# Attention's values in 32-column tiles turned by VectorE, a planner with other durations, and other banks where the channel products change

## The chip, the cores and the metric

The kernel runs on one core of one Trainium2 chip. A core has TensorE (PE) for matrix products, VectorE (DVE), ScalarE (ACT) and GpSimd (POOL) for elementwise work, and SyncE (SP), which here only issues DMAs. Matrix products land in PSUM: 128 partitions by eight banks of 512 fp32 words, addressed in the kernel as `ps[:, bank, column]`. Everything else lies in one SBUF tile called `arena`. The metric is device time in microseconds (us), lower is better; the median of several executions is compared.

## The reference, cut to what matters

```python
batch, n_heads, seq, head_dim = (4, 8, 768, 64);  n_clusters = 16
# routed attention, for each of 32 heads
q_assign = argmax(q_n @ c_n.T);  k_assign = argmax(k_n @ c_n.T)      # nearest centroid
scores = where(q_assign[:, None] == k_assign[None, :], q @ k.T / 8, -1e9)
attn = softmax(scores);  out = attn @ v
# x: (4, 768, 512), the heads side by side; then the mixer
h = relu(x.T @ w_tok1) @ w_tok2          # over tokens, 768 -> 256 -> 768
u = x + h.T
h2 = relu(u @ w_ch1) @ w_ch2             # over channels, 512 -> 1536 -> 512
return u + h2
```

The kernel reads the weights as pairs of 32-bit words (64-bit numbers) and rounds them on the chip; its products are fp32, the mask product bf16.

## The kernel before

**One program, planned.** The kernel first builds a list of operations with `g.add`: each has the engines it may run on with a cost in us for each, a function that issues its instructions, and the SBUF and PSUM pieces it reads and writes. `Program.run` gives each operation a due time, counted back from the TensorE operations that need it, and `Program.plan` then simulates the engines and picks, for each engine, the ready operation with the earliest due time. TensorE's operations stay in the order in which the program lists them; the order on VectorE, ScalarE, GpSimd and SyncE is what the plan yields. The constants `COST`, `LAT`, `LAND` and the costs written at each call are the plan's durations. On the chip each engine works through its list in that order and waits on semaphores.

**Attention** goes by pairs of heads, `m` from 0 to 15 (`NP`), two heads `h` on 64 partitions each. A pair has these steps on TensorE:
- `route(m + 2)`: which centroid each of 384 × 4 queries and keys is nearest to. Four products in 32-column tiles go to one bank; VectorE turns the bank in 32 × 32 blocks, takes maxima, compares and turns back; ScalarE makes a bf16 mask `rb`, which DMAs carry into `Ms`.
- `scores(m)`: 12 units, each of one half `u` of the queries (384 columns) and one block `i` of 128 keys. A unit has an fp32 product and a bf16 mask product per head, in two of the banks 0 to 5 (`2 * s + h`, `s = n % 3`). ScalarE's exponential moves each unit into a buffer `exs`; VectorE adds the exponentials over the blocks of keys into `es`.
- `values(m)`: for each unit and head one product with 64 columns of V as weights and 384 columns of exponentials moving, accumulated in banks 6 and 7 with head 0 on partitions 0 to 63 and head 1 on 64 to 127. So 24 products a pair. ScalarE copies the result to `avs`.
- `sums(m)`: four products with a 32-column matrix of ones give the softmax denominators in bank 5, which are copied to `denS`.
- `finish_x(m)`: nine transposes by TensorE (`turn`), six of `avs` into banks 6 and 7 and three of `denS` into bank 4, so that tokens lie on partitions; VectorE clamps and inverts the denominators and writes the quotient into `xs`, two products of 384 columns.

Beside this, `dma_turn_qk` prepares q and k of pair `m + 3`: ScalarE splits them in 16-bit halves, DMA transposes turn them, ScalarE puts them together again (`halves`). `weight_round` loads a piece of the weights and rounds it on VectorE (31 pieces), and `channel_weights` makes sums of the rounded pieces and stores them in DRAM (`wd1`, `wd2`).

**The mixer** follows: token products (`token1`, `token2`, in Winograd's form of Strassen's scheme with seven products for eight), then `channel1(grp)` and `channel2(grp)` for two groups of two batches. A channel `product` has seven steps of three matmuls; each step's result is taken out of its banks by VectorE, or by ScalarE where it is only copied. `channel1` alternates between banks 0 to 2 and 3 to 5, `channel2` uses one bank a step, chosen by the counter `nset[1]`. Between `channel1(1)` and `channel2(1)` stands `check()`, one tiny product and some vector operations that decide whether a general path has to run. At the end `store` turns four blocks of the output with TensorE, copies them out and sends them.

Two lines that the change touches in many places: TensorE's products all go through the helper `mm` (line 829 of the profile), and elementwise sums through `tt` (line 868), so these lines gather operations of every stage.

Of the kernel before, what the change touches and what calls it, by code (L numbers as in the profile page):

```python
# [14 lines left out]
ALU = mybir.AluOpType  # L15
# [5 lines left out]
P = 128  # L21
# [27 lines left out]
NEX = 11  # L49
# [4 lines left out]
    "ACT": (0.17, 0.00083),  # L54
    "ACT16": (-0.1, 0.00128),
    "DVE": (0.16, 0.00104),
# [8 lines left out]
LAND = 2.2  # L65


class Op:
    __slots__ = ("opts", "fn", "preds", "succs", "left", "ready", "end", "due", "seq", "eng", "lat", "bytes", "after", "port", "first_lat")


class Program:
# [5 lines left out]
    LAT = {"PE": 0.2, "ACT": 0.15, "DVE": 0.12, "POOL": 0.15, "SP": 0.0}  # L78
# [4 lines left out]
    def add(self, opts, fn, rd=(), wr=(), size=None, after=0.0):  # L83
# [3 lines left out]
        o.lat = 0.0  # L87
# [58 lines left out]
    def plan(self):  # L146
# [12 lines left out]
        order, at = [], {}  # L159
        while len(order) < len(ops):  # L160
            best = None
            for e in self.ENGINES:
                if e == "PE":
# [3 lines left out]
                    t = max(free[e], o.ready)  # L167
# [35 lines left out]
            if e == "PE":  # L203
                pe_at += 1
                at[o] = t
# [504 lines left out]
def kernel(  # L710
# [59 lines left out]
    rcps = [Buf(arena, 384 + 32 * i, [HJ, 4]) for i in range(2)]  # L770
    dall = Buf(arena, 448, [NP, HJ, 4])
# [55 lines left out]
    def mm(dst, lhsT, rhs, start, stop, cost, rd, wr, pos=None, tr=None):  # L827
# [6 lines left out]
        return g.add({"PE": cost}, fn, rd, wr)  # L834
# [46 lines left out]
    def vec(fn, c, rd, wr):  # L881
        return g.add({"DVE": c}, lambda e: fn(), rd, wr)
# [129 lines left out]
    def dma_turn_qk(m):  # L1012
# [11 lines left out]
        for n in range(2):  # L1024
            halves(dst[:, :, :, n], qkt[n].ap, 2 * S, qkt[n].k(), T.k())

    def route(m, bk):
# [4 lines left out]
        for gr in range(4):  # L1032
# [3 lines left out]
                T.ap[:, r0 : r0 + HJ].rearrange("p a t -> p (a t)"), True, True, 0.157,  # L1036
# [46 lines left out]
    def scores(m):  # L1083
        nonlocal nex
        T, M = Ts[m % 3], Ms[m % 2]
        st = unit[m] = []

        def plain(n):
            u, i = divmod(n, NJ)
            s, r0 = n % 3, NJ + HJ * u  # L1090
            for h in range(2):
# [3 lines left out]
                    T.ap[hs, r0 : r0 + HJ].rearrange("p a t -> p (a t)"), True, False, 0.316,  # L1095
# [8 lines left out]
        for n in range(2 * NJ):  # L1104
            u, i = divmod(n, NJ)
# [3 lines left out]
            for h in range(2):  # L1109
# [3 lines left out]
                    M.ap[hs, 0, u * HS : (u + 1) * HS], False, True, 0.078,  # L1113
# [3 lines left out]
            ex = exs[nex % len(exs)]  # L1117
            nex += 1
            st.append(ex)
            g.add(  # L1120
                {"ACT": 0.81},
# [783 lines left out]
```

## Time and profile before

| | us |
|---|---|
| median of 3 runs | 812.88 (812.24 to 814.05) |
| the profiled execution | 810.43 |
| its span, first to last instruction | 808.6 |
| TensorE busy | 788.8 (98% of the span) |
| VectorE busy | 672.1 (83%) |
| ScalarE busy | 474.7 (59%) |
| GpSimd busy | 179.3 (22%) |

Attention fills the first 343 us, token mixing follows up to the first "full" channel products, and the rest is channel products. In a row of groups stand the line, the engine, the operation, result and operands, the shape, the count, then busy time, mean duration in ns, and the idle time before with what ended it. In a row of the timeline stand start, duration, and in square brackets the idle time before. "PEld" is TensorE's loading of weights, which can overlap its matmuls; since the ends of matmuls are modelled, the starts tell the pace. A row of windows gives, for each stretch, the busy time of PE, PEld, DVE, ACT and POOL with the number of instructions, then the granted clock, the DMA share and GB/s.

### The profile page before, as it was taken

What the parts mean: (1) busy time and instruction counts of PE and PEld (TensorE: products, weight loads), DVE (VectorE), ACT (ScalarE), POOL (GpSimd) and SP (SyncE); (2) the same over time, 40 slices, a digit from 0 to 9 for tenths busy, and PEclk for the clock granted to TensorE, in tenths of its full rate; (3) what the DMA queues carried; (4) which work ended last, traced back from release to release, by engine and by line L of the source; (5) the groups of instructions that cost most, each with busy time, mean ns of one, the idle gap of its engine ahead of it and who ended that gap; (6) DMA issues with size and microseconds to landing.
All of it is one profiled execution on the core that took longest, in us unless ns stands there. A gap on an engine that the chain in (4) does not pass through costs nothing.

```text
span 808.6 us, 10858 instructions
## 1 busy us (share of the span) xinstructions
PE 788.8 (98%) x3743; PEld 428.0 (53%) x3743; DVE 672.1 (83%) x868; ACT 474.7 (59%) x613; POOL 179.3 (22%) x124
## 2 busy tenths in 40 slices
PE   5999999999999999999999999999999999999996
PEld 3454445444445554444555555555555555555553
DVE  4788999999999999998898876799974676789974
ACT  4588888888888875799913236433455505300423
POOL 1000000000000000000345498500196279610000
PEclk9999999999999999999999999999999999999999
DMA  6777678879887984369839765556899843333656
GB/s 135 225 173 177 181 196 201 219 184 220 198 218 176 231 236 105 90 137 211 146 97 253 208 192 184 177 182 198 243 231 263 220 117 107 89 102 103 177 146 151
DMA packets 265119, 143.49 MB, mean 177 GB/s; under 512 B 184288, under 2 KB 260960, under 8 KB 265056
## 3 DMA queue, kind: packets, MB, share of 16 engines
q1 hardware_dynamic: 262560, 141.88, 68.4%
q10 hardware_dynamic: 2496, 0.84, 0.4%
q8 instruction: 32, 0.52, 0.3%
q14 instruction: 31, 0.25, 0.1%
HBM read 91.95 MB, written 28.61 MB: 149 GB/s over the span
## 4 chain that ended last, share of the span: by engine, by line
PE 96%; DVE 1%; ACT 0%; issue 0%; DMA 0%; SPq 0%; ACTq 0%
PE ps L829 96%; DVE arena L850 0%; DVE arena L868 0%; DMA arena<-arena 0%; ACT arena L875 0%; ACT arena L1122 0%; ACT arena L848 0%; SPq L888 0%; DVE arena L1244 0%; DVE arena L1045 0%; DVE arena L1044 0%; ACTq L848 0%
## 5 line engine op out<-in xcount | busy, mean ns | idle before, releaser
L829 PE MATMUL ps<-arena 128*128 128x384 f32 (+6 forms) x3743 | 788.8, 463 | 12.5 <-DVE arena L981 5.7
L829 PEld LDWEIGHTS ps<-arena 128*128 128x128 f32 (+3 forms) x3359 | 408.6, 168 | 346.9 <-issue 142.6
L868 DVE TENSOR_TENSOR arena<-arena 128x1536 f32<-128x1536 f32 (+6 forms) x351 | 365.7, 1067 | 14.4 <-ACT arena L1122 7.5
L868 POOL TENSOR_TENSOR arena<-arena 128x384 f32<-128x384 f32 (+1 forms) x116 | 175.9, 1547 | 530.7 <-DVE arena L868 396.0
L868 DVE TENSOR_TENSOR arena<-ps,arena 128x384 f32<-128x384 f32 (+2 forms) x259 | 208.0, 810 | 81.5 <-PE ps L829 74.1
L858 ACT COPY arena<-arena 128x768 uint16<-128x768 uint16 (+1 forms) x197 | 191.7, 1050 | 47.0 <-DVE arena L868 29.6
L1122 ACT ACTIVATE arena<-ps 128x768 f32<-128x768 f32 x192 | 150.3, 810 | 16.7 <-PE ps L829 13.2
L848 ACT COPY arena<-ps 128x384 f32<-128x384 f32 (+2 forms) x68 | 45.9, 677 | 133.1 <-PE ps L829 123.1
L1755 ACT ACTIVATE arena<-arena 128x768 f32<-128x768 f32 x40 | 38.7, 967 | 59.8 <-DMA arena<-in_moe_w_ch_dram 43.1
L875 ACT ACTIVATE arena<-arena 128x1152 f32<-128x1152 f32 (+1 forms) x38 | 40.1, 1076 | 55.3 <-DVE arena L868 27.9
L829 PEld LDWEIGHTS <-arena 64*128 64x128 bf16 x384 | 19.3, 94 | 26.3 <-issue 1.8
L850 DVE COPY arena<-ps 128x384 f32<-128x384 f32 (+3 forms) x17 | 12.8, 774 | 15.2 <-PE ps L829 13.5
L1238 DVE SCALAR_TENSOR_TENSOR arena<-arena 128x512 uint32<-128x512 uint32 (+1 forms) x31 | 20.7, 672 | 0.3
L1244 DVE SCALAR_TENSOR_TENSOR arena<-arena 128x512 f32<-128x512 uint32 (+1 forms) x31 | 20.7, 691 | 0.2
L1044 DVE STREAM_TRANSPOSE arena<-ps 128x384 f32<-128x384 f32 x16 | 9.3, 584 | 13.6 <-PE ps L829 13.6
L1053 ACT ACTIVATE arena<-arena 128x384 bf16<-128x384 f32 x16 | 11.2, 703 | 10.3 <-DVE arena L1179 10.3
L1234 DVE TENSOR_SCALAR arena<-arena 128x512 uint32<-128x512 uint32 (+1 forms) x31 | 12.9, 440 | 0.0
L1241 DVE TENSOR_SCALAR arena<-arena 128x512 uint32<-128x512 uint32 (+1 forms) x31 | 12.7, 430 | 0.2
L1049 DVE STREAM_TRANSPOSE arena<-arena 128x384 f32<-128x384 f32 x16 | 9.2, 575 | 0.4
L1045 DVE TENSOR_REDUCE arena<-arena 128x24 f32<-128x384 f32 x16 | 8.8, 553 | 0.6
L1755 ACT ACTIVATION_READ_ACCUMULATOR arena<-arena 128x1 f32 x40 | 7.6, 190 | 0.0
L1186 DVE RECIPROCAL arena<-arena 128x12 f32<-128x12 f32 x16 | 3.6, 228 | 0.6
(47 smaller groups left out, 19.1 us busy)
## 6 DMA issues: line engine op xcount, KB each, us to landing
arena<-wd SPq DMA_DIRECT2D x196, 192.0 KB, 2.4
wd<-arena SPq DMA_DIRECT2D x84, 224.0 KB, 3.7
arena<-in_moe_w_ch_dram SPq DMA_DIRECT2D x48, 256.0 KB, 4.4
arena<-in_moe_w_ch_dram SPq DMA_DIRECT2D x16, 768.0 KB, 4.5
arena<-in_v_dram SPq DMA_DIRECT2D x16, 384.0 KB, 4.4
out_dram<-arena SPq DMA_DIRECT2D x14, 384.0 KB, 3.6
arena<-in_k_dram SPq DMA_DIRECT2D x13, 384.0 KB, 4.4
arena<-in_q_dram SPq DMA_DIRECT2D x13, 384.0 KB, 4.4
```

Source lines behind the costliest of these rows:

```text
L829: nc.tensor.matmul(dst, lhsT=lhsT, rhs=rhs, start=start, stop=stop, tile_position=pos, is_transpose=tr, skip_group_check=True,)
L848: nc.scalar.copy(out=dst, in_=src)
L850: nc.vector.tensor_copy(out=dst, in_=src)
L858: nc.scalar.copy(out=dst, in_=src)
L868: (nc.vector if e == "DVE" else nc.gpsimd).tensor_tensor(out=dst, in0=a, in1=b, op=op)
L875: nc.scalar.activation(out=dst, in_=src, func=ACT.Relu)
L1122: lambda e, ex=ex, s=s: nc.scalar.activation(out=ex.ap, in_=ps[:, 2 * s : 2 * s + 2, 0:HS], func=ACT.Exp, scale=SM_SCALE),
L1234: vec(lambda: nc.vector.tensor_scalar(out=hh, in0=hi, scalar1=0x07FFFFFF, scalar2=3, op0=ALU.bitwise_and, op1=ALU.logical_shift_left,), f, ...
L1238: vec(lambda: nc.vector.scalar_tensor_tensor(out=TT, in0=hi, scalar=0xC0000000, in1=hh, op0=ALU.bitwise_and, op1=ALU.bitwise_or), 0.14 + 0 ...
L1241: vec(lambda: nc.vector.tensor_scalar(out=hh, in0=TT, scalar1=0xFF800000, scalar2=None, op0=ALU.bitwise_and), f, T.k(), h.k())
L1244: vec(lambda: nc.vector.scalar_tensor_tensor(out=ll, in0=lo, scalar=float(2.0**-52), in1=hh.bitcast(F32), op0=ALU.mult, op1=ALU.mult,), 0. ...
L1755: lambda e, i=i, func=func, bias=bias, n=n, hi=hi: nc.scalar.activation(out=hi, in_=hi, func=func, bias=bias, accum_out=wsum.ap[:, i, n : ...
```

## The change

- **Values.** The tile has 32 columns of V instead of 64. For each block `i` there are 16 products: two heads, two halves of 32 channels, and four groups of queries; a group is every fourth run of 32 queries, so 192 columns move in runs of 32. The four groups go to the four 32-partition strips of a bank, so VectorE can turn the result in 32 × 32 blocks straight into `xs`, and `avs` and TensorE's transposes go.
- **Exponentials.** One buffer holds both halves of a block (seven buffers of 2 × 768). From pair 1 on, scores go block by block rather than half by half. `es` holds two partial sums over three blocks each; `sums` adds them in PSUM with eight products.
- **Order.** `route(m + 2)` stands between scores and values for pairs 2 to 13, after the finish for pairs 0 and 1; `sums` stand before the last block of values. The finish of the last pair no longer stands inside token mixing.
- **Planner.** Other costs and latencies, a cost for a change of TensorE's tile form (`SWITCH`), and one between dependent operations of one engine (`SELF`). Piece `n` of the weights may not be loaded before 14 + 12 n us of the plan. `halves` of 1536 elements are split in two.
- **Channel products.** `nset[1]` is set to 3 at the start of each `channel2`, the check's product moves from bank 7 to bank 0, two sums are split in two, and the stores of the last group are issued between the steps of the last product, into banks 4 to 7.

```diff
 COST = {
-    "ACT": (0.17, 0.00083),
-    "ACT16": (-0.1, 0.00128),
-    "DVE": (0.16, 0.00104),
+    "ACT": (0.09, 0.00083),
+    "ACT16": (-0.36, 0.001426),
+    "DVE": (0.075, 0.00104),
     "POOL": (0.12, 0.0023),
 }
+SWITCH = 0.1
+SELF = 0.13
+START, STEP = 14.0, 12
...
-    LAT = {"PE": 0.2, "ACT": 0.15, "DVE": 0.12, "POOL": 0.15, "SP": 0.0}
+    LAT = {"PE": 0.2, "ACT": 0.22, "DVE": 0.2, "POOL": 0.15, "SP": 0.0}
...
-                    t = max(free[e], o.ready)
+                    t = max(free[e] + (SWITCH if o.mode != mode else 0.0), o.ready)
...
-                s.ready = max(s.ready, o.end + (self.delay(o) if s.opts.keys() != {e} or o.lat else 0.03))
+                if e == "PE" and "PE" in s.opts:
+                    d = 0.0
+                elif s.opts.keys() == {e} and not o.lat:
+                    d = SELF if e in ("ACT", "DVE") else 0.03
+                else:
+                    d = self.delay(o)
+                s.ready = max(s.ready, o.end + d)
...
-    exs = [buf(48 + 3 * i, [2, HS]) for i in range(12)]
-    es = [buf(84 + 6 * i, [2, 2, HS]) for i in range(2)]
-    avs = buf(102, [2, HS])
-    denS = buf(105, [HS])
+    exs = [buf(48 + 6 * i, [2, S]) for i in range(6)] + [buf(96, [2, S])]
+    es = [buf(84 + 6 * i, [2, S]) for i in range(2)]
+    denT = buf(105, [HS])
...
-            halves(dst[:, :, :, n], qkt[n].ap, 2 * S, qkt[n].k(), T.k())
+            for r in range(0, NQK, NJ):
+                halves(
+                    dst[:, r : r + NJ, :, n], qkt[n].ap[:, r : r + NJ], S, qkt[n].k(),
+                    T.rows(r, r + NJ),
+                )
...
+        def chunk(n):
+            return divmod(n, NJ) if m == 0 else divmod(n, 2)[::-1]
...
-        for u in range(2):
-            a, e = es[u], st[NJ * u : NJ * u + NJ]
...
-            x, y, z = two(0), two(2), two(4)
-            tt(a.ap, x.ap, y.ap, ALU.add, 4 * HS, x.k() + y.k(), a.k())
-            tt(a.ap, a.ap, z.ap, ALU.add, 4 * HS, a.k() + z.k(), a.k())
-            tt(a.ap[:, 0], a.ap[:, 0], a.ap[:, 1], ALU.add, 2 * HS, a.k(), a.rows(0, 1))
+        for n in range(2):
+            a = es[n]
+            x, y, z = st[HJ * n : HJ * n + HJ]
+            tt(a.ap, x.ap, y.ap, ALU.add, 2 * S, x.k() + y.k(), a.k())
+            tt(a.ap, a.ap, z.ap, ALU.add, 2 * S, a.k() + z.k(), a.k())
...
+    def tokens(ap, gr):
+        return ap.rearrange("p (j t) -> p j t", t=P)[:, :, 32 * gr : 32 * gr + 32]
+
+    def values(m, i):
+        V, ex = vs[m % 3], unit[m][i]
+        mms(
+            [
+                (
+                    ps[32 * gr : 32 * gr + 32, 6 + h, c * HS // 2 : (c + 1) * HS // 2],
+                    V.ap[:, h, i, 32 * c : 32 * c + 32], tokens(ex.ap[:, h], gr),
+                    i == 0 and c == 0, i == NJ - 1, (0, 32 * gr),
+                )
+                for h in range(2) for c in range(2) for gr in range(4)
+            ],
+            1.29, V.k() + ex.k(), bank(6, 7), (P, 32),
+        )
...
     def sums(m, bk):
-        for u in range(2):
...
+        for n in range(2):
+            mms(
+                [
+                    (
+                        ps[32 * gr : 32 * gr + 32, bk, 0:HS], ones.ap,
+                        tokens(es[n].ap.rearrange("p h t -> p (h t)"), gr), n == 0, n == 1,
+                        (0, 32 * gr),
+                    )
+                    for gr in range(4)
+                ],
+                0.645, es[n].k() + ones.k(), bank(bk), (P, 32),
+            )
...
+        vec(lambda: nc.vector.transpose(out=denT.ap, in_=ps[:, bk, 0:HS]), 0.57, bank(bk), denT.k())
...
+        vec(
+            lambda: nc.vector.transpose(
+                out=x.ap[:, :, cols].rearrange("p j (c d) -> p c j d", d=32),
+                in_=ps[:, 6:8, 0:HS],
+            ),
+            0.96, bank(6, 7), xk,
+        )
+        xv = x.ap[:, :, cols].rearrange("p j (h d) -> p j h d", h=2)
+        tt(
+            xv, xv,
+            rcp.ap.rearrange("p h j -> p j h").unsqueeze(3).to_broadcast([P, NJ, 2, D]),
+            ALU.mult, S, xk + rcp.k(), xk,
+        )
+
+    def pair(m):
+        scores(m)
+        early = 2 <= m < NP - 2
+        if early:
             route(m + 2, 0)
-        sums(m, 5)
-        if 3 <= m + 3 < NP:
+        for i in range(NJ):
+            if i == NJ - 1:
+                sums(m, 5)
+            values(m, i)
+        finish_x(m, 5)
+        if m == 0:
+            load_v(2)
+            turn_qk(2, (1, 2, 3))
+        if m < 2:
+            route(m + 2, 0)
+        if m + 3 < NP:
             dma_turn_qk(m + 3)
...
+        after = START + STEP * npiece
         raw, (h, T, low) = raws[npiece % 3], tmps[npiece % 2 if npiece < 22 else 0]
...
-    nset = [0, 3]
+    nset = [0, 0]
...
+            for late in dict(then).get(n, ()):
+                late()
...
+        nset[1] = 3
         product(2, 2, Hm[1, 1], u[0, 1], u[0, 1], ("POOL",))
...
-        product(2, 3, Hm[1, 0], u[1, 0], u[1, 0])
+        stores = [
+            lambda f=f, hf=hf: store(grp, 0, f, hf) for f, hf in ((2, 1), (3, 1), (2, 0), (3, 0))
+        ]
+        then = {4: stores[0:1], 5: stores[1:2], 6: stores[2:4]} if grp else {}
+        product(2, 3, Hm[1, 0], u[1, 0], u[1, 0], then=then)
...
-        bk, o, queue = 2 + nost, ost[nost], ("SP", "ACT")[nost % 2]
+        bk, o, queue = 4 + nost, ost[nost], ("SP", "ACT")[nost % 2]
...
-        mm(ps[0:32, 7, 0:3], ones.ap, cnt.ap[:, 0:3], True, True, 0.1,
-           cnt.k() + ones.k(), bank(7), pos=(0, 0))
+        mm(ps[0:32, 0, 0:3], ones.ap, cnt.ap[:, 0:3], True, True, 0.1,
+           cnt.k() + ones.k(), bank(0), pos=(0, 0))
...
-    finish_x(NP - 1, (6, 7), 4)
```

More of the change, by code (lines that the diff above doesn't have):

```diff
@@ L48 @@
 W = 64
-NEX = 11
 SUM_LO, SUM_HI = 1e-15, 1e15
@@ L1602, in product @@
         )
-        for pn, (r, rk), st, fresh, part, more in seq:
+        for n, (pn, (r, rk), st, fresh, part, more) in enumerate(seq):
             w = ring[nring % len(ring)]
@@ L1819 @@
     for m in range(NP):
[L1820 to L1825 removed]
+        pair(m)
     load_token_weights()
```

165 lines of the change are left out of this document (60 added, 105 removed).

## The prediction

> **What bounds the kernel now.** I read the page first: its busy rows, the slices, the chain that ended last.
>
> ```profile
> PE 788.8 (98%) x3743; PEld 428.0 (53%) x3743; DVE 672.1 (83%) x868; ACT 474.7 (59%) x613; POOL 179.3 (22%) x124
> PE   5999999999999999999999999999999999999996
> PEclk9999999999999999999999999999999999999999
> PE 96%; DVE 1%; ACT 0%; issue 0%; DMA 0%; SPq 0%; ACTq 0%
> ```
>
> TensorE sets the time: 98% busy, 96% of the chain, its clock full. So an edit is worth what it takes out of TensorE's stream, and work of other engines counts only where it makes TensorE wait. "Busy" hides small losses, because the ends of matmuls are modelled and overlap; I therefore go by the starts of weight loads in the timeline. One pair of heads in mid-attention:
>
> ```profile
> 182.51 0.30 PEld L829 LDWEIGHTS ps<-arena 64*128 64x128 f32 x4 [0.17 <-issue]
> ...
> 192.40 0.20 PEld L829 LDWEIGHTS ps<-arena 128*64 128x64 f32 x4 [0.48 <-DVE arena L868]
> 192.78 0.14 PEld L829 LDWEIGHTS ps<-arena 128*64 128x64 f32 x2 [0.18 <-issue]
> ...
> 199.55 0.14 PEld L829 LDWEIGHTS ps<-arena 128*64 128x64 f32 x2 [0.18 <-issue]
> ...
> 200.29 0.16 PEld L829 LDWEIGHTS ps<-arena 128*32 128x32 f32 x8 [0.60 <-ACT arena L858]
> 200.46 0.80 ACT L848 COPY arena<-ps 128x768 f32<-128x768 f32 x1 [0.21 <-ACT arena L858]
> 200.64 0.13 PEld L829 LDWEIGHTS ps<-arena 128*32 128x32 f32 x4 [0.19 <-DVE arena L1241]
> 200.97 0.13 PEld L829 LDWEIGHTS ps<-arena 128*32 128x32 f32 x4 [0.19 <-issue]
> 201.21 0.58 DVE L1044 STREAM_TRANSPOSE arena<-ps 128x384 f32<-128x384 f32 x1 [0.75 <-PE ps L829]
> 201.72 1.03 PEld L829 LDWEIGHTS ps<-arena 128*128 128x128 f32 x9 [0.62 <-ACT arena L848]
> ...
> 202.92 0.30 PEld L829 LDWEIGHTS ps<-arena 64*128 64x128 f32 x4 [0.17 <-issue]
> ```
>
> The pair lasts 202.92 − 182.51 = 20.41 us: scores 9.89, values in 64-column tiles 7.89, route and sums in 32-column tiles 1.43, nine turns 1.20. Each part includes the step into the next form of tile. These parts are what the change rewrites.
>
> **The pace of small tiles.** The row of the value matmuls by form, and the token stage's 512-column stream:
>
> ```profile
> L829 PE MATMUL ps<-arena 128*64 128x384 f32 x768 | 127.4, 488 | 0.0
> 344.00 0.19 PEld L829 LDWEIGHTS ps<-arena 128*128 128x128 f32 x1 [0.24 <-issue]
> ...
> 347.86 0.19 PEld L829 LDWEIGHTS ps<-arena 128*128 128x128 f32 x1 [0.24 <-issue]
> ```
>
> The code issues 16 pairs × 24 = 384 value matmuls and the row has 768, so an fp32 matmul is two instructions. Two 64-column tiles run side by side: from 192.78 to 199.55 lie 21 steps, 0.3224 us for 384 columns. Between 344.00 and 347.86 lie nine steps of 512 columns, 0.4289. The slope is (0.4289 − 0.3224)/128 = 0.00083 us a column, the fixed part 0.003. Four 32-column tiles side by side (a quad, four instructions) also step by 0.33 for 384 columns (200.64 to 200.97). So a quad of 192 columns should take 192 × 0.00083 + 0.003 = 0.1626 us.
>
> **The change part by part, on TensorE.**
> - Values: 16 matmuls a block, six blocks a pair: 6 × 16 × 2 / 4 = 48 quads × 0.1626 = 7.80 us, against 24 steps × 0.3224 = 7.74. The cost is even (+0.06), though instructions go from 48 to 192 per pair.
> - Sums: eight matmuls of 384 columns instead of four, because VectorE no longer adds the two halves: four quads instead of two, 1.29 instead of 0.645 us.
> - Turns: nine a pair go, 1.20 us with the step out of them.
> - Form steps: values, sums and early route now share the 32-column form. A step costs 200.29 − 199.55 = 0.74 for two quads of work, 0.74 − 2 × 0.322 = 0.10; the 32-column part ends 1.43 − 4 × 0.3224 = 0.14 late, step out included. Two steps remain of four.
> - New pair: 9.89 + 0.645 (route) + 7.80 + 1.29 + 0.14 = 19.77 us, against 20.41: −0.64. Twelve pairs (2 to 13) have this form: −7.7 us.
> - Pairs 0 and 1 route after the finish, into bank 0, which the next scores write first. VectorE's reading transpose started 0.24 us after route's stream (201.21 against 200.97) and took 0.58; with the return about 0.9 us lies open, which sums and turns covered before. Each pair: −0.64 + 0.90 = +0.26, together +0.5.
>
> The last two pairs and the edges of the later stages:
>
> ```profile
> 304.97 0.30 PEld L829 LDWEIGHTS ps<-arena 64*128 64x128 f32 x4 [0.17 <-issue]
> 324.90 0.30 PEld L829 LDWEIGHTS ps<-arena 64*128 64x128 f32 x4 [0.17 <-issue]
> 343.46 0.30 PEld L829 LDWEIGHTS ps<-arena 128*128 128x128 f32 x2 [0.62 <-issue]
> 701.00 1.36 DVE L868 TENSOR_TENSOR arena<-ps,arena 128x1152 f32<-128x1152 f32 x1 [0.58 <-PE ps L829]
> 702.83 0.14 PEld L829 LDWEIGHTS ps<-arena 128*32 128x32 f32 x2 [0.55 <-issue]
> 703.37 1.41 DVE L868 TENSOR_TENSOR arena<-ps,arena 128x1152 f32<-128x1152 f32 x2 [1.01 <-PE ps L829]
> 704.83 1.53 PE L829 MATMUL ps<-arena 128*128 128x384 f32 x4 [1.78 <-issue]
> 799.90 1.23 PEld L829 LDWEIGHTS ps<-arena 128*128 128x128 f32 x11 [0.18 <-issue]
> 800.10 0.56 DVE L868 TENSOR_TENSOR arena<-ps,arena 128x384 f32<-128x384 f32 x1 [1.38 <-PE ps L829]
> 800.57 1.94 DVE L850 COPY arena<-ps 128x384 f32<-128x384 f32 x4
> ```
>
> - Pair 14 has no route: 19.93 becomes 9.89 + 7.80 + 1.29 + 0.14 = 19.12, −0.8. Pair 15 took 18.56, plus its nine turns inside token mixing (about 1.0 by the 1.03 of nine): 19.6 becomes 19.12, −0.4.
> - Banks: before the last channel2 TensorE does the check's matmul at 702.83 and then waits until VectorE has emptied banks 3 to 5, which ends just before 704.83. With `nset[1] = 3` the first product takes banks 6 and 7 and the check bank 0, which is emptied at 702.36. Of the 2.0 us some 0.3 stay for the check: −1.7.
> - End: two of the four stores move between the last product's steps. Their six turns (about 0.65 us) move ahead of the last matmul, which then ends that much later; the last add (0.56), turn and copy stay in a row behind it, where four copies waited before. 0.65 + about 2.3 against about 2.9: zero. Less traffic with the last two stores may give up to −1; I take 0.
>
> **The other engines.** Durations by form:
>
> ```profile
> L868 DVE TENSOR_TENSOR arena<-arena 128x1536 f32<-128x1536 f32 x84 | 148.1, 1766 | 10.9 <-ACT arena L1122 7.5
> L868 DVE TENSOR_TENSOR arena<-arena 128x768 f32<-128x768 f32 x32 | 30.6, 958 | 1.1
> L868 DVE TENSOR_TENSOR arena<-ps,arena 128x384 f32<-128x384 f32 x170 | 92.5, 554 | 32.6 <-PE ps L829 25.4 <-ACT arena L858 0.2
> L1044 DVE STREAM_TRANSPOSE arena<-ps 128x384 f32<-128x384 f32 x16 | 9.3, 584 | 13.6 <-PE ps L829 13.6
> 180.00:200.00 20.00, 20.00 (x145) 10.02 (x143) 18.21 (x27) 17.59 (x22) 0.00 (x0) 1.00 0.89 220
> ```
>
> VectorE loses, per pair, two 768-column adds (1.92 us) and two 384-column products from PSUM (1.11). It gains a transpose of the sums (0.58), one of the values (768 columns, not in the trace: at least 0.58, at most twice that, 1.17; I take 0.99 since part is fixed) and a 768-column product (0.96): 2.53 against 3.03. ScalarE loses the 0.80 copy at 200.46 and mostly the one of the sums; its 1536-element halves become two of 768. Costed at nothing: the new VectorE work runs under the next scores. Tightest is the sums' transpose, which must leave bank 5 before the third score unit: values of the last block (1.30) and two units (9.89/12 = 0.8 each) cover it, 2.9 us for 0.24 + 0.58. Without cover it costs 0.9 a pair. Values' banks 6 and 7 have the whole scores (9.89) for about 2.1 us of transposing and waiting. The early route gives up nothing: bank 0 is free once the tenth exponential is done, and the mask has a pair more time. No DMA is added; weight loads only take other places in SyncE's queue, spread by `START` and `STEP`, and the channel products need the last of them after attention. POOL idles here (0.00 in the window).
>
> **Sum.** −7.7 + 0.5 − 0.8 − 0.4 − 1.7 = −10.1 us. The profiled execution took 810.43 (span 808.6 and 1.8 around it), so 800.3 like it; the median, 812.88, stands 2.4 higher and gives **802.8**.
>
> **The rivals.**
> *A, weight loads come out from under the short quads (slower).* There are 16 × 48 = 768 quads. The nearest rows: the first quad after a form step took 200.64 − 200.29 = 0.35 instead of 0.32, so a load that has to be waited for shows 0.025 at least; a group of four loads lasts 0.13. Bounds: 0 to 0.13 × 768 = +100 us; by the nearest row +19 us, that is 822. It decides from 10.1/768 = 0.013 us a quad. For it: no 192-column fp32 stream and no moving operand in runs of 32 is in the trace. Against: at 200.64 the four loads of the next quad are done by 200.77, well before a start 0.16 later, and the 384-column quads show no trace of them.
> The Trainium skill (TensorE: Matmul & The Clock Gate, Part 3: Packing small matmuls — row/col tiling) says that a weight load overlaps running matmuls only where the row group differs; here all four tiles use all rows, so by it every quad would pay its loads, the +100 us end. The 0.33 step at 200.64 with four loads inside contradicts that, and I leave it a small part of A.
>
> *B, VectorE becomes the bound (slower).* In the window it is busy 18.2 of 20 us. The rounding of the weights and the sums over them:
>
> ```profile
> L1238 DVE SCALAR_TENSOR_TENSOR arena<-arena 128x512 uint32<-128x512 uint32 (+1 forms) x31 | 20.7, 672 | 0.3
> L1244 DVE SCALAR_TENSOR_TENSOR arena<-arena 128x512 f32<-128x512 uint32 (+1 forms) x31 | 20.7, 691 | 0.2
> L1234 DVE TENSOR_SCALAR arena<-arena 128x512 uint32<-128x512 uint32 (+1 forms) x31 | 12.9, 440 | 0.0
> L1241 DVE TENSOR_SCALAR arena<-arena 128x512 uint32<-128x512 uint32 (+1 forms) x31 | 12.7, 430 | 0.2
> L868 DVE TENSOR_TENSOR arena<-arena 128x448 f32<-128x448 f32 x48 | 29.2, 616 | 0.0
> L868 DVE TENSOR_TENSOR arena<-arena 128x512 f32<-128x512 f32 x35 | 23.6, 701 | 0.4
> L868 DVE TENSOR_TENSOR arena<-arena 128x256 f32<-128x256 f32 x48 | 18.7, 419 | 0.4
> ```
>
> Together 138.5 us, 8.7 a pair. Pair work will be about 11.9 us (four 1536-column adds 7.06, route's four passes at about 0.58, the 2.53 above). If the new planner put all rounding inside attention, that is 20.6 against 19.77: TensorE waits 0.8 a pair, and with the idle 1.8 of 20 that VectorE shows today up to 2.6; I take 1.2, 20 us in all: 820. It decides from 0.63 a pair. Against: the old demand (8.98 of adds, 2.3, 1.5, 8.7 = 21.5) was further above its 20.41, and what did not fit ran after attention.
>
> *C, new small waits eat part.* The order on every engine is planned anew. 0.1 to 0.5 us a pair returned gives 804.5 to 811; at 0.63 the change does nothing.
>
> **Chances.** Main sum 0.66 (799 to 806: quads without fixed cost −2, stores −1, a few waits +3); C, still faster, 0.10; within 0.2% 0.04; A 0.10; B 0.10. So faster 0.76, same 0.04, slower 0.20; 0.2% (1.6 us) is about what runs of this kernel can tell. The range 799 to 814 holds the main case, C, no change and the mild ends of A and B.
>
> **What would show it.** Score starts 19.8 us apart; 32-column loads every 0.16 within values; two form steps a pair; nothing of the nine turns; TensorE going on within 0.4 us of the check. Wrong if quads step by 0.18 or more (A), if pairs are uneven with gaps ahead of scores or values put down to DVE (B), or if pairs shrink and later stages grow.

## The result, and the profile after

The changed kernel took 817.36 us (median of 6 runs, 816.35 to 820.19) against 812.70 for the kernel before on the same chip: a ratio of 1.0051, with a 95% interval of 1.0037 to 1.0066. So it is slower by half a per cent, where 802.8 and a range of 799 to 814 were forecast. The profiled execution has a span of 814.7 us, 6.1 more than before; the prediction's sum, −10.1 on the span of 808.6, stood for 798.5. So 16.2 us have to be found.

The page of the kernel after: its busy row and the chain that ended last.

```profile
PE 790.0 (97%) x6031; PEld 464.4 (57%) x6031; DVE 656.4 (81%) x848; ACT 455.8 (56%) x615; POOL 178.5 (22%) x124
...
PE 86%; ACT 7%; DVE 2%; issue 1%; DMA 1%; SPq 0%; ACTq 0%; DVEq 0%
```

The busy share of TensorE is only one point lower. The chain shows the change: ScalarE had 0% of it and now has 7%, about 57 us of the span on which the end hangs by ScalarE, although ScalarE itself became less busy (474.7 before, 455.8 now). The rows of waits say for what TensorE stands still (total us, number, longest); the first is from the kernel before, the second from the kernel after. L1122 and L1137 are the same exponential.

```profile
PEld ps L829 <- ACT arena L1122: 5.6, 22, 1.0
```

```profile
PEld ps L838 <- ACT arena L1137: 31.6, 81, 1.0
```

These totals hold the ordinary pause ahead of each load too (0.22 or so), so the number of waits says more than their sum. Where in the pair they lie is read from the timeline of the kernel after (start, duration, engine, line, operation, count, and in brackets the idle time before it with what ended it). This is one pair, from its first score to the next pair's first:

```profile
205.71 0.30 PEld L838 LDWEIGHTS ps<-arena 64*128 64x128 f32 x4 [0.30 <-issue]
...
210.99 0.30 PEld L838 LDWEIGHTS ps<-arena 64*128 64x128 f32 x4 [0.71 <-ACT arena L1137]
...
215.45 0.30 PEld L838 LDWEIGHTS ps<-arena 64*128 64x128 f32 x4 [0.70 <-ACT arena L1137]
...
216.46 0.16 PEld L838 LDWEIGHTS ps<-arena 128*32 128x32 f32 x8 [0.48 <-ACT arena L1137]
...
226.33 0.30 PEld L838 LDWEIGHTS ps<-arena 64*128 64x128 f32 x4 [0.30 <-DVE arena L1204]
```

The part in 32-column tiles, route, values and sums, lasts 226.33 − 216.46 = 9.87 us. The prediction's 0.645 + 7.80 + 1.29 + 0.14 is 9.875. The scores, which the change hardly touches, last 216.46 − 205.71 = 10.75, not 9.89. Two loads in them start after a pause of 0.71 and 0.70 instead of 0.22, and both pauses are ended by an exponential. What the exponentials were late for is on ScalarE's own timeline, in the same pair:

```profile
206.83 2.49 ACT L1137 ACTIVATE arena<-ps 128x768 f32<-128x768 f32 x3 [1.42 <-PE ps L838]
209.21 1.06 ACT L867 COPY arena<-arena 128x768 uint16<-128x768 uint16 x1
210.12 3.66 ACT L1137 ACTIVATE arena<-ps 128x768 f32<-128x768 f32 x5
213.68 1.05 ACT L867 COPY arena<-arena 128x768 uint16<-128x768 uint16 x1
214.59 2.91 ACT L1137 ACTIVATE arena<-ps 128x768 f32<-128x768 f32 x4
217.36 3.06 ACT L867 COPY arena<-arena 128x768 uint16<-128x768 uint16 x4
...
224.55 1.99 ACT L867 COPY arena<-arena 128x768 uint16<-128x768 uint16 x2 [1.59 <-DMA arena<-arena]
227.45 1.62 ACT L1137 ACTIVATE arena<-ps 128x768 f32<-128x768 f32 x2 [0.90 <-PE ps L838]
228.96 1.05 ACT L867 COPY arena<-arena 128x768 uint16<-128x768 uint16 x1
```

Twice, at 209.21 and 213.68, a 16-bit copy stands between two exponentials and holds the next one back by 0.91 us. Exponentials follow each other by about 0.71 (210.12 to 213.68 for five) and TensorE needs one per 0.81, so each exponential makes good only 0.1. TensorE is at most three units ahead (three slots of two banks), and so it runs into the late exponential three units on. The copies turn q and k of a later pair. Their whole way is in this view and in SyncE's. Four copies split the halves (217.36) and two DMA transposes follow. Four copies then put the halves back: two at 224.55, one at 228.96, and one five exponentials later in the same scores (as at 213.68, a pair earlier). The copies back can't stand ahead of the end of `scores(m)`: they write the `T` of pair `m + 3`, of which there are three buffers, so it is the one that `scores(m)` reads.

```profile
219.71 3.33 SPq L902 DMA_TRANSPOSE arena<-arena  x2
```

The two issues keep SyncE busy from 219.71 to 223.04, and the first result is used at 224.55, 4.8 us after the issue began. By the same 4.8 the second, issued from about 221.3 on, should be there at about 226 (an estimate), and the first two copies back end at 226.54. So the third can't run before the next scores begin at 226.33.

**Where the 6.1 us and the 16.2 us lie.** Starts of pairs 2 and 14 and of the 512-column stage, before, after:

```profile
60.05 0.30 PEld L829 LDWEIGHTS ps<-arena 64*128 64x128 f32 x4 [0.17 <-issue]
```

```profile
62.01 0.19 PEld L838 LDWEIGHTS ps<-arena 64*128 64x128 f32 x2 [1.62 <-DVE arena L1057]
...
278.67 0.14 PEld L838 LDWEIGHTS ps<-arena 128*32 128x32 f32 x4 [0.97 <-ACT arena L1137]
279.61 0.14 PEld L838 LDWEIGHTS ps<-arena 128*32 128x32 f32 x4 [0.80 <-ACT arena L867]
...
310.07 0.30 PEld L838 LDWEIGHTS ps<-arena 64*128 64x128 f32 x4 [0.30 <-DVE arena L1197]
348.31 0.30 PEld L838 LDWEIGHTS ps<-arena 128*128 128x128 f32 x2 [0.30 <-issue]
```

| us | before | forecast | after |
|---|---|---|---|
| start of pair 2 | 60.05 | 60.55 | 62.01 |
| twelve pairs, 2 to 13 | 244.92 | 237.2 | 248.06 |
| pairs 14 and 15 | 38.49 | 38.24 | 38.24 |
| end of attention | 343.46 | 336.1 | 348.31 |
| from there to the end of the span | 465.1 | 462.4 | 466.4 |

Of the 16.2 us, some 12.2 lie within attention: 10.8 in the twelve pairs, whose mean is 20.67 instead of 19.77, and about 1.5 ahead of pair 2. In pairs 2 and 12 route itself waited for a copy as well: at 279.61 its second half starts 0.94 after the first, released by L867. The other 4.0 us lie behind attention. The bank gain came: the check's load at 709.45 and those of the next product are one unbroken run, and that product starts at 709.60, 0.15 later, where it took 2.00 before.

```profile
709.45 1.74 PEld L838 LDWEIGHTS ps<-arena 128*32 128x32 f32 x8 [0.55 <-DVE arena L877]
```

But token mixing and the first channel products, from the end of attention to the check, take 2.8 us more than forecast (361.1 us; 359.4 before, less 1.0 for the moved turns), in many small waits. From the last step's first load (805.18; 799.90 before) to the end of the span it is 9.5 us against 8.7.

### The profile page after: what moved, and what is told of

The parts are those of the page before. It is cut to its first block, busy times and chain, and to the rows that moved or that the text cites. A ratio compares the mean times of both kernels' runs of the same rounds, so it can differ in the third digit from the quotient of the medians.

```text
span 814.7 us, 15363 instructions
## 1 busy us (share of the span) xinstructions
PE 790.0 (97%) x6031; PEld 464.4 (57%) x6031; DVE 656.4 (81%) x848; ACT 455.8 (56%) x615; POOL 178.5 (22%) x124
## 4 chain that ended last, share of the span: by engine, by line
PE 86%; ACT 7%; DVE 2%; issue 1%; DMA 1%; SPq 0%; ACTq 0%; DVEq 0%
PE ps L838 68%; PE ps L1153 18%; ACT arena L867 3%; ACT arena L1137 3%; DVE arena L877 2%; ACT arena L857 0%; DMA arena<-wd 0%; ACT arena L884 0%; DVE arena L1270 0%; DMA arena<-arena 0%; DVE arena L1273 0%; DVE arena L1057 0%; SPq L897 0%; DVE arena L1209 0%; DVE arena L859 0%
## 5 line engine op out<-in xcount | busy, mean ns | idle before, releaser
L838 PE MATMUL ps<-arena 128*128 128x384 f32 (+4 forms) x2703 | 645.3, 468 | 16.5 <-DVE arena L990 5.7
L838 PEld LDWEIGHTS ps<-arena 128*128 128x128 f32 (+2 forms) x2319 | 335.7, 184 | 274.5 <-issue 59.5
L877 DVE TENSOR_TENSOR arena<-arena 128x1536 f32<-128x1536 f32 (+6 forms) x339 | 352.6, 1061 | 31.6 <-ACT arena L1137 22.0
L877 POOL TENSOR_TENSOR arena<-arena 128x384 f32<-128x384 f32 (+1 forms) x116 | 175.1, 1536 | 539.4 <-ACT arena L867 388.6
L877 DVE TENSOR_TENSOR arena<-ps,arena 128x384 f32<-128x384 f32 (+2 forms) x227 | 189.7, 845 | 93.6 <-PE ps L838 89.7
L867 ACT COPY arena<-arena 128x768 uint16<-128x768 uint16 x223 | 195.9, 949 | 68.3 <-DMA arena<-arena 43.6
L1137 ACT ACTIVATE arena<-ps 128x768 f32<-128x768 f32 x192 | 144.2, 819 | 30.2 <-PE ps L838 29.8
L1153 PE MATMUL ps<-arena 128*32 128x192 f32 (+1 forms) x3328 | 149.7, 338 | 0.0
L1153 PEld LDWEIGHTS ps<-arena 128*32 128x32 f32 x3328 | 109.6, 110 | 41.1 <-issue 14.4
L857 ACT COPY arena<-ps 128x1152 f32<-128x1152 f32 (+2 forms) x44 | 32.0, 731 | 117.4 <-PE ps L838 117.2
L1209 DVE STREAM_TRANSPOSE arena<-ps 128x768 f32<-128x768 f32 x16 | 15.6, 977 | 0.8 <-PE ps L1153 0.7
L1195 DVE STREAM_TRANSPOSE arena<-ps 128x384 f32<-128x384 f32 x16 | 9.3, 582 | 7.1 <-PE ps L1153 7.0
L1057 DVE STREAM_TRANSPOSE arena<-ps 128x384 f32<-128x384 f32 x16 | 9.2, 576 | 5.5 <-PE ps L838 5.3
```

Of the source, the lines that this page charges most:

```text
L838: nc.tensor.matmul(dst, lhsT=lhsT, rhs=rhs, start=start, stop=stop, tile_position=pos, is_transpose=tr, skip_group_check=True,)
L857: nc.scalar.copy(out=dst, in_=src)
L867: nc.scalar.copy(out=dst, in_=src)
L877: (nc.vector if e == "DVE" else nc.gpsimd).tensor_tensor(out=dst, in0=a, in1=b, op=op)
L1137: lambda e, ex=ex, s=s, u=u: nc.scalar.activation(out=ex.ap[:, :, u * HS : (u + 1) * HS], in_=ps[:, 2 * s : 2 * s + 2, 0:HS], func=ACT.Exp ...
L1153: nc.tensor.matmul(dst, lhsT=lhsT, rhs=rhs, start=start, stop=stop, tile_position=pos, skip_group_check=True,)
```

## The experiments

Every kernel was timed against the kernel before on the same chip. "S" in the expectations is the first theory, in which the cheaper plan cost of the exponential (0.70, was 0.81) lets the planner slip copies in; "R" is the one formed when S fell.

| label | median us | ratio to before, 95% | end of attention, us |
|---|---|---|---|
| (after) | 817.36 | 1.0051, 1.0037–1.0066 | 348.3 |
| exp81 | 839.76 | 1.0316, 1.0289–1.0343 | 372.0 |
| hold | 829.78 | 1.0208, 1.0177–1.0239 | 361.5 |
| old_planner | 838.95 | 1.0305, 1.0275–1.0335 | 372.2 |
| planner_only | 831.00 | 1.0222, 1.0197–1.0247 | 357.0 |
| late_hold | 809.02 | 0.9934, 0.9910–0.9958 | 339.6 |
| late2_hold | 808.23 | 0.9912, 0.9881–0.9944 | 338.1 |
| late_only | 817.06 | 1.0032, 1.0020–1.0043 | 348.1 |
| early_before | 835.14 | 1.0246, 1.0219–1.0273 | 363.3 |
| stale_hold | 809.36 | 0.9955, 0.9938–0.9971 | 336.1 |
| pair1_inside | 805.89 | 0.9909, 0.9889–0.9929 | 338.9 |
| no_metering | 812.21 | 0.9991, 0.9978–1.0003 | 339.8 |
| banks_only | 813.49 | 1.0004, 0.9993–1.0015 | 343.4 |

**First, the planner.** Two ways to keep the copies out of the exponentials, the whole planner of before under the new structure, and the new planner under the old structure.

```diff
# exp81 (in the kernel after)
-                {"ACT": 0.70},
+                {"ACT": 0.81},
# hold (in the kernel after)
-HOLD = {"DVE": 0.15}
+HOLD = {"DVE": 0.15, "ACT": 0.15}
```

> The changed kernel with one number different: the plan's cost of an exponential, 0.81 instead of 0.70 us, so that the plan finds no idle moment of ScalarE between exponentials to put a 16-bit copy in. Theory S (slipped copies): the scores stall because copies of about 0.9 us stand between exponentials in ScalarE's list. Then the scores part falls from about 10.6 to 9.9-10.0 us, score starts come 19.8-20.0 apart, and the time falls by 8 to 10 us to 806-810. Theory D (the block-by-block order with seven buffers makes exponentials wait for buffers or for VectorE): no planner cost helps, scores stay at 10.4-10.7, time 815-819.

> The changed kernel with all its planned durations, but ScalarE may wait up to 0.15 us in the plan for an operation that is due earlier. Theory S: copies leave the first eight units of the scores, as with the dearer exponential; scores 9.9-10.0, time 806-810. Theory D: 815-819.

> The changed kernel (tiles, order, banks, stores) with the planner's durations and latencies of before, no cost for a change of tile form, no metering of the weights. Theory S, which puts the loss on the planner's new durations and not on the tiles: scores 9.9-10.0 in nearly all pairs, time 803-810, faster than before. If the structure itself loses (theory D): 815 or more.

> The kernel before with the new planner alone (durations, latencies, form cost, metered weights), no other edit. Theory S: some copies slip between exponentials, fewer than in the changed kernel since a copy still has 1536 elements in half the cases; scores longer in those pairs by 0.3 each or more, time 813-818. Theory D: equal to before, 811.5-813.5.

Theory S missed all four: the first three by 20 us and more, planner_only by 13. Theory D's times were passed too, but for its "815 or more" of old_planner; that the structure itself is not what costs is seen below, where the same buffers run at the full pace. Theory S was right on one thing: in exp81 the scores of all twelve pairs run clean, and in hold those of seven. From the start of the first matmul to that of the last they take 9.64 us, as in the kernel before. But nothing was won by it, since the wait went to the next place. The timeline of hold, TensorE's loads at the end of the scores and ScalarE beside it:

```profile
199.32 0.14 PEld L838 LDWEIGHTS ps<-arena 128*32 128x32 f32 x4 [0.70 <-ACT arena L1137]
200.26 0.14 PEld L838 LDWEIGHTS ps<-arena 128*32 128x32 f32 x4 [0.80 <-ACT arena L867]
```

```profile
190.32 7.33 ACT L1137 ACTIVATE arena<-ps 128x768 f32<-128x768 f32 x9 [0.64 <-PE ps L838]
197.54 1.05 ACT L867 COPY arena<-arena 128x768 uint16<-128x768 uint16 x1
198.46 0.81 ACT L1137 ACTIVATE arena<-ps 128x768 f32<-128x768 f32 x1
199.15 1.06 ACT L867 COPY arena<-arena 128x768 uint16<-128x768 uint16 x1
```

Nine exponentials now run undisturbed. The last two copies stand at 197.54 and 199.15. The first holds back the tenth exponential, which empties the bank that route writes: route starts at 199.32, when it is done (198.46 + 0.81). Route's second half starts at 200.26, when the copy of 199.15 is done. In exp81 four copies stand there instead of two, two on each side of the tenth exponential, and the price is larger: 2.54 us here for the first half alone. First ScalarE, then TensorE's load:

```profile
195.32 7.33 ACT L1137 ACTIVATE arena<-ps 128x768 f32<-128x768 f32 x9 [5.29 <-PE ps L838]
202.55 1.96 ACT L867 COPY arena<-arena 128x768 uint16<-128x768 uint16 x2
205.06 1.97 ACT L867 COPY arena<-arena 128x768 uint16<-128x768 uint16 x2
```

```profile
206.16 0.14 PEld L838 LDWEIGHTS ps<-arena 128*32 128x32 f32 x4 [2.54 <-ACT arena L867]
```

Here ScalarE stands idle for 5.29 us ahead of the first exponential. The two transposes were issued from 188.13 on, so by the 4.8 us above the first was done at about 193 (an estimate): part of this price is the order that the plan chose. old_planner loses in the same place as hold: in all its twelve pairs TensorE pauses for 1.5 to 2.7 us ahead of route, and most pairs last 22.6 us, as the last ones of hold do.

So with route early the copies found no good place: ahead of the tenth exponential they stall the scores (0.86 in the pair shown of the kernel after), beside or behind it they stall route (1.1 to 2.9 us a pair in hold). From this came theory R: the early route of the pair after next sets a deadline that the copies meet in none of these plans. And planner_only shows that the new constants cost 2.2% even in the structure of before, where route is late. Not all of that is copies among exponentials: in one pair TensorE waited for the mask's DMA (3.62 and 0.99 us), and this pair alone is 5.9 us long of the 13.5 that attention lost.

**Second, the early route.** It is moved within the values, with and without ScalarE's hold, and made alone in the kernel before.

```diff
# late_hold, late_only (in the kernel after; late2_hold has NJ - 2)
-        if early:
-            route(m + 2, 0)
         for i in range(NJ):
+            if early and i == NJ - 1:
+                route(m + 2, 0)
# late_hold and late2_hold besides
+HOLD = {"DVE": 0.15, "ACT": 0.15}
# early_before (in the kernel before)
         scores(m)
+        if 2 <= m < NP - 2:
+            route(m + 2, 0)
...
-        if 2 <= m + 2 < NP:
+        if m + 2 < NP and not 2 <= m:
             route(m + 2, 0)
```

> The changed kernel with route(m + 2) of pairs 2 to 13 moved from behind the scores to just ahead of the last block of values, and ScalarE allowed to wait 0.15 us in the plan. Theory R (the early route is what costs: it reads q and k of pair m + 2, whose last 16-bit copies on ScalarE cannot run before the scores of pair m, so they either stand between exponentials or hold route up): with some 6.5 us more until route the copies run behind the last exponential and nobody waits. Scores 9.9-10.1, values with sums and route 9.9, score starts 19.8-20.0 apart; attention ends near 335 instead of 348, time 801-807, faster than both kernels. If the loss is instead a lack of ScalarE time in any order, or buffers: 812 or more.

> The same with route one block earlier (ahead of the fifth of six blocks, 1.3 us less until route). Theory R: two copies of 0.95 us behind the last exponential, which ends about 1 us after the scores, are done some 3 us after the scores, route comes after 5.2 us: still free, 801-807. If the margin were smaller than I think, route would wait: 810-820.

> Late route without the wait in the plan. Theory R with theory S: the plan still fills idle moments between exponentials with copies, about 20 in the middle of scores against some 27 before; each costs 0.3 us. Scores 10.1-10.6, time 808-815. If the early route alone were the cause: 801-807, as with the wait.

> The kernel before with one edit: route(m + 2) of pairs 2 to 13 between scores and values. Theory R: route then needs copies of 1.9 us each that the old plan ran at the end of the scores and behind them, so TensorE waits 1 to 4 us in each of twelve pairs ahead of values: 825-850. If the early route is free, as predicted: 811-815.

late_hold and late2_hold came out 1 to 2 us above the 801 to 807 expected, late_only 2 above its range; early_before lies within its own. Place of route and order on ScalarE make a square of four, as ratios to the kernel before: early without hold 1.005, early with hold 1.021, late without hold 1.003, late with hold 0.993. Neither move does anything good alone; both together give 1.2%. On one chip, late with hold is 8.0 us faster than late without. The waits behind the exponential, of late_only and late_hold:

```profile
PEld ps L838 <- ACT arena L1137: 29.1, 73, 1.6
```

```profile
PEld ps L838 <- ACT arena L1137: 4.3, 13, 1.1
```

Late alone leaves the copies where the plan had put them, amid the exponentials. With the hold they move behind the ninth or tenth. In late2_hold, ScalarE and TensorE:

```profile
201.19 7.33 ACT L1137 ACTIVATE arena<-ps 128x768 f32<-128x768 f32 x9 [0.70 <-PE ps L838]
208.41 1.05 ACT L867 COPY arena<-arena 128x768 uint16<-128x768 uint16 x1
209.32 0.81 ACT L1137 ACTIVATE arena<-ps 128x768 f32<-128x768 f32 x1
210.01 2.96 ACT L867 COPY arena<-arena 128x768 uint16<-128x768 uint16 x3
212.82 1.52 ACT L1137 ACTIVATE arena<-ps 128x768 f32<-128x768 f32 x2
```

```profile
61.72 0.19 PEld L838 LDWEIGHTS ps<-arena 64*128 64x128 f32 x2 [1.62 <-DVE arena L1057]
...
209.96 5.03 PEld L1153 LDWEIGHTS ps<-arena 128*32 128x32 f32 x128 [0.48 <-DVE arena L877]
215.02 0.29 PEld L838 LDWEIGHTS ps<-arena 128*32 128x32 f32 x8
...
298.89 0.19 PEld L838 LDWEIGHTS ps<-arena 64*128 64x128 f32 x2 [0.30 <-DVE arena L1062]
338.10 0.30 PEld L838 LDWEIGHTS ps<-arena 128*128 128x128 f32 x2 [0.30 <-issue]
```

The last two exponentials are 2.8 us late here and it costs nothing: all scores are out by then, and their readers are the sums and the last block of the values. Route (215.02, eight loads in one run) waits for nothing. Twelve pairs take 298.89 − 61.72 = 237.17, 19.76 each, the forecast 19.77. In early_before, where nothing but route's place changes in the code, a 1536-element copy stands in the same way ahead of the ninth exponential. The scores stand still because of it, and the kernel loses 2.5%; pairs are 21.4 to 22.0 long instead of 20.41, the first 23.5.

```profile
201.49 1.90 ACT L858 COPY arena<-arena 128x1536 uint16<-128x1536 uint16 x1
```

```profile
204.11 0.30 PEld L829 LDWEIGHTS ps<-arena 64*128 64x128 f32 x4 [1.56 <-ACT arena L1122]
```

**Third, the reason itself and the remaining parts.** stale_hold leaves route early and the hold in, but lets route read q and k of the pair before its own, which were long turned (so the clusters of twelve pairs aren't those of the reference). The deadline goes and TensorE's work stays the same; the order of the other engines is planned anew with it. pair1_inside takes late2_hold and routes in pair 1 as in the others. no_metering takes late2_hold without the spreading of the weight pieces. banks_only puts the banks, the check's bank and the stores between the steps into the kernel before.

```diff
# stale_hold (with hold)
-            route(m + 2, 0)
+            route(m + 2, 0, m + 1)
# pair1_inside (with late2_hold)
-        early = 2 <= m < NP - 2
+        early = 1 <= m < NP - 2
...
-        if m < 2:
+        if m < 1:
             route(m + 2, 0)
# no_metering (with late2_hold)
-        after = START + STEP * npiece
# banks_only (in the kernel before), its core
-    nset = [0, 3]
+    nset = [0, 0]
...
+        nset[1] = 3
         product(2, 2, Hm[1, 1], u[0, 1], u[0, 1], ("POOL",))
```

> The changed kernel with the wait of 0.15 us in ScalarE's plan and route left early, where it stood, but route of pair m + 2 reads the q and k of pair m + 1, which are ready (so twelve pairs get the wrong clusters; TensorE's and VectorE's instructions are the same in number and size). Theory R (only the readiness of q and k of pair m + 2 makes the early place dear): pairs of 19.8 us, time 803-810, against 829.8 for the same kernel with the right q and k. If the place itself costs (bank 0, VectorE's four passes, the mask's DMAs): 820-830.

> The version with route ahead of the fifth block, and pair 1 treated like pairs 2 to 13 instead of routing behind its finish. By the prediction's term for a route behind the finish (0.9 us open ahead of the next scores) pair 1 becomes about 1 us shorter (20.76 to 19.8), all else equal: 807 against 808.2. If q and k of pair 3 are late there, nothing or a loss.

> The version with route ahead of the fifth block, weight pieces allowed as early as before (30 us, and 180 us for the second channel weights) instead of one in 12 us of the plan. If metering keeps VectorE free for attention: score starts become uneven, 810-815. If it only pushes rounding into the token and channel stages, where this version loses about 3 us more than the kernel before: 803-807.

> The kernel before with the new banks, the check's product in bank 0 and the stores between the last product's steps, nothing else. By the prediction: the 2.0 us ahead of the last channel2 shrink to 0.2-0.3, the end is unchanged: 1.5 to 2 us faster, 812.5 against 814.4. If the stores lengthen the end, as the changed kernel's tail suggests (9.8 us from the last matmul of the products to the end against 9.0): no difference.

stale_hold decides it. Against hold one argument of the code differs, and attention ends 25.4 us sooner, on the forecast's 336.1:

```profile
336.09 0.30 PEld L838 LDWEIGHTS ps<-arena 128*128 128x128 f32 x2 [0.30 <-issue]
```

Its whole stays above the forecast (a span of 806.9 against 798.5): 8.4 us are lost behind attention, some 6 of them in four gaps between matmul starts (at 406.9, 410.5, 422.5 and 703.7), each 1.1 to 1.9 us longer than the usual 0.16. pair1_inside shows what the open route of pair 1 was worth: that pair takes 62.05 − 42.28 = 19.77, against 20.76 in late2_hold, so 0.99 where the forecast had 0.9.

```profile
42.28 0.30 PEld L838 LDWEIGHTS ps<-arena 64*128 64x128 f32 x4 [1.40 <-DVE arena L1057]
62.05 0.30 PEld L838 LDWEIGHTS ps<-arena 64*128 64x128 f32 x4 [0.30 <-issue]
```

It has the lowest median of all, 805.89, and beats both kernels; late2_hold's interval overlaps it, and attention ended no sooner (pair 0 and pair 15 had new stalls of 1.7 and 1.4 in their scores). no_metering came out as the first of its two branches said: 812.21, 4 us above late2_hold, and the intervals don't meet. Five of its twelve pairs are longer than 19.76, by up to 1.9 us, four of them at the end of attention, which ends 1.7 us later; the loads of values waited for VectorE's additions 7.2 us in ten places, against 3.3 in eight in late2_hold. Where the rest lies is open, for the profile is of the fastest of its ten runs (a span of 806.6; late2_hold has 806.2). banks_only is no different from before. The 2.0 us at the check come (the next product starts 0.16 behind it) and go again: TensorE then waits 1.6 us at the next product, where VectorE does a sum of 3.73 us ahead of the additions out of PSUM that would free the bank. First the loads at the check and TensorE behind it, then VectorE:

```profile
702.77 1.10 PEld L829 LDWEIGHTS ps<-arena 128*32 128x32 f32 x6 [0.55 <-DVE arena L868]
```

```profile
708.67 2.50 PE L829 MATMUL ps<-arena 128*128 128x384 f32 x7 [1.61 <-issue]
```

```profile
704.38 3.73 DVE L868 TENSOR_TENSOR arena<-arena 128x1152 f32<-128x1152 f32 x1
708.03 1.01 DVE L868 TENSOR_TENSOR arena<-ps,arena 128x384 f32<-128x384 f32 x2
```

That this sum is what TensorE waits for is read from the order of the rows; it wasn't tried with the sum elsewhere. The same stall stands in exp81, old_planner, late_only, late2_hold and stale_hold, and not in the kernel after, hold, late_hold, pair1_inside and no_metering, which all have the new banks: the planned order decides whether it comes.

## Why the prediction was wrong

- **The step that failed:** "The early route gives up nothing: bank 0 is free once the tenth exponential is done, and the mask has a pair more time". This stands among the things "costed at nothing", and of ScalarE's work the prediction says only what it loses. The step looked at what route writes and who reads that, not at what it reads. q and k of the pair after next come out of a chain of copies, DMA transposes and copies that takes 9.2 us from 217.36 to 226.5 for its first half alone, and the room between two pairs' scores is 9.87. Before, route stood at the pair's end and the last copies back could run behind the scores (the 1536-element copies of the kernel before). Put early, it needs them before the values, where they stand among the exponentials or hold route up. The term was zero; it measured 2.5% alone in the kernel before (early_before) and 25.4 us of attention between hold and stale_hold, which has the forecast's 336.1. In the kernel after, the twelve pairs lost 10.8 us to this and to the next cause together; the runs don't part them there.
- **A second cause on top, which only rival C touched, with 0.1 to 0.5 us a pair:** the new plan takes an exponential for 0.70 us beside a score unit of 0.807, so it sees idle moments on ScalarE ahead of each exponential and fills them with copies of 0.94. late_only (817.1) against late_hold (809.0) shows that this order does the damage alone too; in planner_only such copies stand among the exponentials of the old structure as well. That it is the 0.70 that opens the moments is read from exp81, where they are gone; with route late it was not tried. The two don't add up: with either one left in, nothing is won.
- **Twelve pairs at 19.77:** the terms were right to 0.01 where the copies were out of the way (19.76 in late2_hold). Quads of 192 columns, the four quads of sums, form steps and pairs 14 and 15 (38.24) came as worked out; in the kernel after, too, the 32-column part has its 9.87 in ten of the twelve pairs.
- **Pairs 0 and 1, "about 0.9 us lies open":** 0.99 in pair 1. The 1.5 us ahead of pair 2 were mainly a later start of the scores, 1.06 us, and a stall of 0.5 in pair 1's.
- **Banks, −1.7:** right at the check (2.00 to 0.15), but it is no gain on the whole by itself (banks_only 1.0004).
- **End, "zero":** the turns moved ahead cost 0.5 (0.65 in the sum), but the tail behind the last step's first load, which was to be 0.65 shorter, is 0.8 longer: 1.3 in all. From the end of VectorE's last copy (806.58 + 0.56) to the end of the span there are 7.6 us, against 6.1 before. Over all the kernels here this tail lies between 4.8 (exp81) and 9.7 (early_before, with the stores of before), so it is not shown that the moved stores make it longer; why it varies stays open. Open as well is which part of the change makes the 2.8 us of small waits in the stages ahead of the check: the whole order is planned anew, and they were not taken apart.
- **Rivals:** A (weight loads) is out, as the 9.87 shows. B (VectorE as the bound) is out for this change: late2_hold runs at the full pace with VectorE's new work in place. Only without the spreading of the weights (no_metering) do waits for VectorE come back. C, "new small waits", was nearest, with its point of no gain at 0.63 a pair; the waits were 0.90. The rival went no further than that point, and it named no engine whose order could cost more.

ScalarE was overlooked because it was idle. It is still: in a window of one pair of the kernel after it is busy 15.71 of 20 us (the columns are PE, PEld, DVE, ACT and POOL, then clock and DMA share), less than the 17.59 of before.

```profile
207.50:227.50 20.00, 19.69 (x286) 11.90 (x284) 18.96 (x29) 15.71 (x23) 0.00 (x0) 1.00 0.90 216
```

What sets the wait is the order of its work, not the amount: late2_hold does the same copies and exponentials, and its twelve pairs last 19.76 each.

## What to carry to other kernels

When a step moves earlier, follow each of its inputs back to where it starts, through copies and DMAs on other queues, and compare that chain with the new room; that the outputs' buffers are free says only half. An engine with a fifth of its time free can still set the pace if one 0.9 us instruction lands between two that another engine waits for every 0.8 us: ask in which gaps the work may stand at no cost, here behind the last score unit, and give the planner that rule. A planner's durations are part of the kernel: ones nearer the trace (0.70 for exponentials that follow each other by 0.71) made the plan tighter and the kernel slower, until the fillers were held back and the deadline moved.

## What the runs showed of the hardware

- Four 32-column tiles side by side run 192-column fp32 streams with every weight load hidden. Values, sums and route are 54 quads in 9.87 us; with 0.3225 for each of the six of 384 columns and 0.14 for the form steps, 48 quads are left with 7.80, 0.1624 each. The Trainium skill (TensorE: Matmul & The Clock Gate, Part 3: Packing small matmuls — row/col tiling) has a load overlap only where the row group differs. Here all tiles use all rows, and the trace disagrees with it, at half the stream length that the prediction could show.
- 16-bit copies of 128x768 on ScalarE follow each other by 0.73 us when they split the halves (four in 3.06 at 217.36) and by 0.94 when they put them back (two in 1.99 at 224.55, each about 1.05 long); the plan has one price for both, 0.735.
- A DMA transpose holds SyncE's queue for 1.2 to 3.3 us (86 of them in the kernel after, median 1.3; 3.33 for the two at 219.71), where the plan has 0.63 for an issue.
- VectorE's transpose of 128x768 out of PSUM took 0.98 us and that of 128x384 0.58 (a fixed part and 0.4 us for 384 columns); the prediction took 0.99.

```profile
L1209 DVE STREAM_TRANSPOSE arena<-ps 128x768 f32<-128x768 f32 x16 | 15.6, 977 | 0.8 <-PE ps L1153 0.7
```
